# Attention units of eight heads and DMA transposes in a fused adaLN transformer layer on one NeuronCore

## The chip, the cores and the metric

The kernel runs on one core of a Trainium2 chip. The metric is the device time of one execution in microseconds (us). A core has a matrix engine (PE, with its weight loads shown as PEld), a vector engine (DVE), a scalar engine (ACT), a general engine (POOL), a queue engine that issues DMA transfers (SP), and 16 DMA engines that carry them. ACT can issue DMA transfers too, on a queue of its own.

## The reference

One transformer layer on 2,048 tokens of 1,024 features in bf16, with scales and shifts (`sa, ca, ga, sb, cb, gb`) made from a condition vector `c`. Attention has 32 query heads of 32 features and a single key and value head.

```
mod = silu(c) @ w_mod                       # six fields of 1024
h   = layernorm(x) * (1 + ca) + sa
q   = h @ wq (32 heads of 32); k = h @ wk; v = h @ wv      # one k and v for all heads
o   = softmax(q k^T / sqrt(32)) v
x   = x + ga * (o @ wo)
h   = layernorm(x) * (1 + cb) + sb
x   = x + gb * ((silu(h @ w1) * (h @ w3)) @ w2)            # 3584 hidden features
```

## The kernel before

**Tiles and blocks.** Tokens are cut into 16 tiles of 128 for the first norm and for keys and values, and into 8 blocks of 256 queries (`NB`, `B`). The 1,024 query features are 8 chunks `f` of 128, so a chunk holds four heads.

**Start.** For every token tile, `lnt1` takes statistics (bn_stats on DVE), makes 1/sigma on POOL, normalizes on ACT (tiles 0 to 7) or DVE (8 to 15) into one of three slots `XN`, transposes the tile on PE by eight 128x128 matmuls and evicts it to `HT` on ACT or DVE. `mod_cols` makes the first scale and shift from `w_mod` (tile `WM0`), `scale0` folds the scale into `wk`, `wv` and the first two chunks of `wq` (`WQ0S`), `k_bias` and `q_bias` make the biases that come from the shift. `k_proj(j)` makes the keys of 256 tokens (`KT`), `v_proj` the values, `q_proj` the query chunks (`QT`). The rest of `wq` (`WQ1`) is scaled in place on DVE once it has landed. All large loads are issued by SP, in an order written out by hand: x tiles 0-7, half of WM0 and the first chunks of `wq` first; then x tiles 8-11, the rest of WM0 (field 0), `WQ1`, x tiles 12-15; then `wo` (`WO`, it waits for `WQ1` to land) and chunks of `w_mod` (tile W2S in the profile).

**Attention.** A step works on one query chunk of a block (four heads) and two key tiles: eight score matmuls of 256 columns on four 32-row parts of PE (`s_exp`), then two exponentials of 128x1024 on ACT into a ring `U` of ten steps. A unit is one chunk, eight steps. `av` adds the 16 key tiles of exponentials on DVE (`pairs` adds two key tiles of two steps, then further additions halve what is left, tile PS), multiplies the exponentials with V (eight matmuls of 256 columns per step on four 32-column parts of PE) and the sums with ones (the denominators), and normalizes: a transpose, a copy, a reciprocal, a transpose back and a product, all on DVE. The result overwrites the query chunk in `QT`.

**The rest of the layer.** For each finished block `wo` multiplies with `wo`, adds x and takes the second norm, whose transposes are done by DMA for blocks 1 to 6; `slab` (14 per block) makes the gated hidden features, with a tanh on ACT and two products on DVE; `quarter` (4 per block) makes the output. This work on block n fills PE while the exponentials of block n+1 run.

**Order.** Nothing is ordered by hand after recording. `op` records an operation with its planned cost and what it reads and writes; `Placer` then lists operations engine by engine: of those that could start about now it takes the one with the earliest due time `vt`. `PLAN` holds one row for every 16 score steps: tolerances, and shifts of the due times by kind of operation. PE distinguishes three modes (scores `S`, attention-value `A`, dense `F`). Within an engine instructions run strictly in the placed order. All instructions are recorded by one helper, so the profile gives them all one line (L22), and tiles tell them apart.

Of the kernel before, what the change touches and what calls it, by code (L numbers as in the profile page):

```python
# [42 lines left out]
class Graph:  # L43
# [63 lines left out]
    def alias(self, new, old):  # L107
# [8 lines left out]
    (0.2, 0.03, 0.0, 0, 1.4,  # L116
     {"q/pe": -9, "slab/act": -80, "wo/dve": -71, "ln/pe": -112, "ln/act": 31, "k/pe": 3, "k/dve": 33}),
    (0.0, 0.12, 0.2, 1, 0.2,
     {"av/pe": -2, "q/pe": -9, "pair/dve": -2, "av/dve": -33, "slab/act": -18, "ln/pe": -57, "ln/act": 23}),
    (0.0, 0.16, 0.02, 0, 0.7, {"wo/pe": 106, "q/pe": -45, "q/dve": -74, "ln/pe": -118, "ln/dve": 4, "mod/pe": -24}),  # L120
    (0.0, 0.16, 0.02, 0, 0.7, {"wo/pe": 106, "q/pe": -45, "q/dve": -74, "ln/pe": -118, "ln/dve": 4, "mod/pe": -24}),
    (0.2, 0.24, 0.2, 1, 0.6, {"q/pe": 47, "mc/pe": 46, "ln/act": -12, "k/pe": 22}),
    (0.0, 0.12, 0.2, 0, 1.8,
     {"wo/pe": -44, "quarter/pe": 47, "q/pe": 33, "mc/pe": 36, "pair/dve": -14, "wo/dve": -1, "ln/act": -12,
      "k/pe": 22}),
    (0.0, 0.11, 0.2, 1, 1.5, {"q/pe": 47, "mc/pe": 46, "av/dve": 6, "ln/act": -12, "k/pe": 22}),
    (0.0, 0.11, 0.2, 1, 1.9, {"q/pe": -13, "mc/pe": 46, "av/dve": 4, "ln/act": -12, "k/pe": 22}),
    (0.0, 0.11, 0.2, 0, 3.4, {"wo/pe": 35, "an/dve": 55, "slab/dve": 1}),
    (0.0, 0.11, 0.2, 1, 1.4, {"av/dve": -11, "an/dve": 55, "slab/dve": 1, "q/dve": 9}),
    (0.0, 0.11, 0.1, 0, 2.4,  # L130
     {"wo/pe": 14, "slab/pe": 12, "quarter/pe": 3, "q/pe": -6, "av/dve": 18, "an/dve": 69, "slab/act": -1,
      "quarter/dve": -7}),
    (0.0, 0.11, 0.05, 0, 2.4, {"slab/act": 6, "wo/dve": 53}),
    (0.0, 0.11, 0.2, 0, 2.9, {"wo/pe": 46, "an/dve": 55, "slab/dve": -89, "q/dve": 67}),
    (0.0, 0.11, 0.2, 1, 1.3, {"wo/pe": -13, "pair/dve": 6, "an/dve": 55, "slab/dve": -89, "q/dve": 67}),
    (0.0, 0.11, 0.1, 1, 2.7,
     {"slab/pe": -132, "q/pe": 47, "mc/pe": 46, "pair/dve": -13, "av/dve": 23, "slab/dve": -39, "slab/act": -20,
      "quarter/dve": -47, "ln/act": -12, "k/pe": 22}),
    (0.0, 0.11, 0.1, 1, 2.3,
     {"slab/pe": -132, "q/pe": 47, "mc/pe": 46, "pair/dve": -13, "av/dve": -84, "slab/act": -20,  # L140
      "quarter/dve": -47, "ln/act": -12, "k/pe": 22}),
# [3 lines left out]
    (0.0, 0.11, 0.2, 1, 1.3,  # L145
     {"slab/pe": -124, "q/pe": 47, "mc/pe": 46, "pair/dve": -24, "av/dve": -89, "an/dve": -26, "slab/dve": -39,
      "slab/act": -20, "ln/act": -12, "k/pe": 22}),
    (0.0, 0.11, 0.05, 1, 3.7,
     {"wo/pe": -5, "quarter/pe": 48, "pair/dve": -3, "av/dve": -2, "slab/act": -7, "wo/dve": 20}),
    (0.0, 0.11, 0.05, 1, 3.7,  # L150
     {"wo/pe": -5, "quarter/pe": 48, "pair/dve": -3, "av/dve": -2, "slab/act": -7, "wo/dve": 20}),
# [4 lines left out]
    (0.0, 0.11, 0.2, 1, 1.3,  # L156
     {"slab/pe": -124, "quarter/pe": 26, "q/pe": 52, "mc/pe": 46, "pair/dve": 13, "av/dve": -72, "an/dve": -26,
      "slab/dve": -39, "slab/act": -20, "quarter/dve": 35, "wo/dve": -6, "ln/act": -12, "k/pe": 22}),
    (0.0, 0.11, 0.05, 1, 2.6,
     {"slab/pe": -124, "quarter/pe": 26, "q/pe": 20, "mc/pe": 46, "av/dve": -89, "slab/dve": -39,  # L160
      "slab/act": -20, "quarter/dve": 35, "ln/act": -12, "k/pe": 22}),
    (0.0, 0.11, 0.05, 1, 1.4,
     {"slab/pe": -124, "quarter/pe": 26, "q/pe": 20, "mc/pe": 5, "av/dve": -89, "slab/act": -20,
      "quarter/dve": 35, "ln/act": -12, "k/pe": 22}),
    (0.0, 0.11, 0.2, 0, 1.6, {"wo/pe": 74, "pair/dve": 40, "av/dve": -2, "an/dve": 55, "slab/dve": -102, "q/dve": 6}),
    (0.0, 0.11, 0.2, 1, 1.4, {"wo/pe": -13, "pair/dve": 40, "av/dve": -2, "an/dve": 55, "slab/dve": -88}),
    (0.0, 0.11, 0.05, 1, 1.9,
     {"slab/pe": -124, "quarter/pe": -21, "q/pe": 20, "mc/pe": 46, "pair/dve": 43, "av/dve": -89,
      "slab/dve": -39, "slab/act": -20, "quarter/dve": 35, "ln/act": -12, "k/pe": 22}),
    (0.0, 0.11, 0.05, 1, 1.9,  # L170
     {"slab/pe": -124, "quarter/pe": -21, "q/pe": 20, "mc/pe": 46, "pair/dve": 43, "av/dve": -89,
      "slab/act": -20, "quarter/dve": 35, "ln/act": -12, "k/pe": 22}),
    (0.0, 0.11, 0.2, 0, 3.4, {"wo/pe": 61, "q/pe": -20, "pair/dve": 3, "slab/dve": -23, "wo/dve": 33}),
    (0.0, 0.11, 0.2, 1, 1.4, {"wo/pe": -5, "quarter/pe": 48, "pair/dve": -20, "av/dve": -27, "slab/act": -7}),
    (0.0, 0.11, 0.05, 0, 2.1,
     {"slab/pe": -124, "quarter/pe": -21, "q/pe": 20, "mc/pe": 46, "pair/dve": 43, "av/dve": -89,
      "slab/dve": -39, "slab/act": -20, "quarter/dve": 35, "q/dve": -75, "ln/act": -12, "k/pe": 22}),
    (0.0, 0.11, 0.05, 0, 4.0,
     {"slab/pe": -124, "quarter/pe": -21, "q/pe": 20, "mc/pe": 46, "pair/dve": 43, "av/dve": -89,
      "slab/act": -20, "quarter/dve": 35, "q/dve": -75, "ln/act": -12, "k/pe": 22}),  # L180
    (0.0, 0.11, 0.2, 0, 3.7,
     {"wo/pe": -4, "slab/pe": -43, "q/pe": 20, "mc/pe": 46, "pair/dve": 43, "av/dve": 55, "slab/dve": -39,
# [4 lines left out]
class Placer:  # L187
# [121 lines left out]
    def commit(self, n, e, k, start):  # L309
# [11 lines left out]
        if e == "sp" or n.dma is not None:  # L321
            self.t[e] = start + dur
            self.bw = max(self.bw, start + 2.6) + n.nbytes / n.bw
            n.fin = self.bw + 0.5
# [119 lines left out]
def build(nc, x_in, wq_in, wk_in, wv_in, wo_in, w1_in, w3_in, w2_in, c_in, wmod_in, out, S, D, F):  # L444
# [34 lines left out]
    RB = sb("RB", [P, 2, B], F32)  # L479
# [9 lines left out]
    RC = sb("RC", [P, 8], F32)  # L489
# [8 lines left out]
    Uf = U[:].rearrange("p a b c d -> p (a b c d)")  # L498
    HTf = HT[:].rearrange("p a b -> p (a b)")
# [16 lines left out]
    GP = HTf[:, o:o + 1024].rearrange("p (s x) -> p s x", s=2)  # L516
# [10 lines left out]
           W2f[:, 0:NC * 512].rearrange("p (c f) -> p c f", c=NC)]  # L527
# [48 lines left out]
    def x_dma(tt0, cnt, vt):  # L576
# [5 lines left out]
        dma("sp", dst, x2[tt0 * P:(tt0 + cnt) * P, :].rearrange("(t p) d -> p t d", p=P), ("XL", tt0),  # L582
            cnt * P * D * 2, writes=keys, vt=vt, bw=FAST)
# [8 lines left out]
    def wq_dma(f0, f1, key, vt):  # L592
        dma("sp", WQ[:, :, f0 * P:f1 * P], cp(wq_in)[:, :, f0 * P:f1 * P], key, (f1 - f0) << 18, writes=[key], vt=vt,
            bw=FAST)
# [61 lines left out]
    def lnt1(tt, vt):  # L656
# [13 lines left out]
        static = tt < 6  # L670
# [138 lines left out]
    def mod_chunk(i, vt):  # L809
# [4 lines left out]
        if i == 1:  # L814
            G.alias([("WMB", 1)], [("XS", tt) for tt in range(6, 10)])
# [31 lines left out]
    CYC = [(n, f, j) for n in range(NB) for f in range(NC) for j in range(NJ)]  # L847
    exps = {}

    def s_exp(c):  # L850
        G.tag = "s"
        n, f, j = CYC[c]
# [8 lines left out]
        op("pe", mm, 0.2184, reads=[("KT", j), ("QT", n, f)], writes=bk, vt=TOP + c, mode="S", post=0.171)  # L861
# [8 lines left out]
    def pairs(c):  # L870
        G.tag = "pair"
        m = c % NU
        op("dve", lambda: [lambda e: e.tensor_tensor(PS[:, c % NP:c % NP + 2], U[:, m:m + 2, :, 0, :],
                                                     U[:, m:m + 2, :, 1, :], ALU.add)], 1.12,
           reads=[("U", m + k, i) for k in range(2) for i in range(2)],
           writes=[("PS", (c + k) % NP) for k in range(2)], vt=c + 101.0, post=0.08)
# [348 lines left out]
```

## Time and profile before

| What | Value |
|---|---|
| Time, median of 3 runs | 1134.34 us (1134.11 to 1134.49) |
| The profiled execution: its own time | 1134.47 us |
| Its span in the trace | 1132.6 us |
| Exponentials on ACT | 1,024 of 128x1024, 964.3 us busy |
| DVE additions of exponentials (`pairs`) | 256 of 128x2048, 1,214 ns each |
| DVE additions of sums | 368 of 128x1024, 684 ns each |
| Input and weight traffic | 209.47 MB, 185 GB/s on average |
| Granted PE clock | full in all 40 slices |

Busy times of neighbouring instructions overlap in this profile: the interval from one start to the next on an engine is shorter than the duration of one (an exponential lasts 1,111 ns and starts 904 ns after the one before). Where the text speaks of a cost in a row of instructions, it means the interval. In a wait, the name behind the arrow is what the waiting engine's next instruction needed last.

### The profile page before, as it was taken

How to read it: one execution, taken by the hardware profiler on the slowest of the kernel's cores; microseconds unless marked ns; L12 is line 12 of the kernel's file. 1: busy time of each engine (PE TensorE's matmuls, PEld its weight loads, DVE VectorE, ACT ScalarE, POOL GpSimd, SP SyncE). 2: the span in 40 equal slices, each digit the busy share in tenths (PEclk: the TensorE clock that was granted, in tenths of full speed). 3: DMA queues.
4: the chain of work that ended last, by engine and by line, in shares of the span. 5: the costliest groups of instructions: out<-in, count | busy, mean ns of one | idle time of the engine just before them, and what ended most of it. 6: DMA issues, size and time to landing. Idle time of an engine off the chain costs nothing.

```text
span 1132.6 us, 34805 instructions
## 1 busy us (share of the span) xinstructions
PE 1113.1 (98%) x15600; PEld 754.6 (67%) x15600; DVE 951.9 (84%) x1544; ACT 1026.0 (91%) x1165; POOL 53.8 (5%) x95
## 2 busy tenths in 40 slices
PE   7999999999999999999999999999999999999998
PEld 6643546666577656776567756776577657766887
DVE  7888899989988888888988998888988988888442
ACT  6999999999999999999999999999999999996110
POOL 5100000000100001000100000000100000000000
PEclk9999999999999999999999999999999999999999
DMA  9500379665596667766596658765696559667793
GB/s 344 184 2 1 114 225 242 186 196 151 129 263 194 173 166 209 208 191 165 141 262 192 174 148 237 196 193 142 173 248 195 160 146 238 190 185 209 217 296 116
DMA packets 374292, 209.47 MB, mean 185 GB/s; under 512 B 17536, under 2 KB 365952, under 8 KB 374144
## 3 DMA queue, kind: packets, MB, share of 16 engines
q1 hardware_dynamic: 373712, 207.11, 65.8%
q8 instruction: 123, 2.02, 0.8%
q14 instruction: 25, 0.20, 0.1%
q10 hardware_dynamic: 432, 0.13, 0.0%
HBM read 199.89 MB, written 4.19 MB: 180 GB/s over the span
## 4 chain that ended last, share of the span: by engine, by line
PE 63%; ACT 31%; DVE 4%; DMA 1%; issue 0%; POOL 0%; SPq 0%; DVEq 0%
PE PB L22 47%; ACT U L22 30%; PE S L22 16%; DVE PS L22 2%; DMA W<-in_A_wq_dram 1%; ACT HT L22 1%; DVE HT L22 1%; DVE RB L22 0%; SPq L22 0%; DVE ST L22 0%; DVE W L22 0%; ACT XNB L22 0%; POOL PS L22 0%; DVE XNB L22 0%; POOL RS L22 0%
## 5 line engine op out<-in xcount | busy, mean ns | idle before, releaser
L22 ACT ACTIVATE U<-S 128x1024 bf16<-128x1024 f32 x1024 | 964.3, 1111 | 9.0 <-PE S L22 8.8
L22 DVE TENSOR_TENSOR PS<-U 128x2048 bf16<-128x2048 bf16 x256 | 309.7, 1214 | 11.7 <-ACT U L22 10.3
L22 DVE TENSOR_TENSOR PS<-PS 128x1024 bf16<-128x1024 bf16 x368 | 249.5, 684 | 4.7
L22 PE MATMUL PB<-QT,W 128*128 128x256 bf16 x1856 | 229.6, 273 | 0.0
L22 PE MATMUL S<-QT,KT 32*128 32x256 bf16 x4096 | 203.5, 273 | 6.0 <-ACT U L22 4.0
L22 PEld LDWEIGHTS PB<-QT,W 128*128 128x128 bf16 x1856 | 170.3, 98 | 46.6 <-issue 28.3
L22 PE MATMUL PB<-W2S,HT 128*128 128x256 bf16 x1512 | 189.1, 273 | 0.0
L22 PEld LDWEIGHTS PB<-W2S,HT 128*128 128x128 bf16 x1512 | 137.5, 98 | 42.4 <-issue 26.4
L22 PEld LDWEIGHTS S<-QT,KT 32*128 32x128 bf16 x4096 | 60.8, 92 | 132.7 <-ACT U L22 118.7
L22 PE MATMUL PB<-U,V 128*32 128x256 bf16 x4032 | 123.5, 273 | 0.0
L22 PE MATMUL PB<-QT,HT 128*128 128x256 bf16 x960 | 119.9, 273 | 0.0
L22 PEld LDWEIGHTS PB<-U,V 128*32 128x32 bf16 x4032 | 100.8, 97 | 18.8 <-issue 7.0
L22 ACT ACTIVATE HT<-PB 128x512 bf16<-128x512 f32 (+1 forms) x110 | 77.6, 707 | 32.0 <-PE PB L22 31.8
L22 PEld LDWEIGHTS PB<-QT,HT 128*128 128x128 bf16 x960 | 88.2, 98 | 23.7 <-issue 14.1
L22 PE MATMUL PB<-HT,W 128*128 128x256 bf16 (+1 forms) x576 | 101.8, 318 | 1.0 <-DVE HT L22 0.6
L22 DVE SCALAR_TENSOR_TENSOR HT<-HT,PB 128x512 bf16<-128x512 bf16 x102 | 69.4, 681 | 34.2 <-ACT HT L22 33.4
L22 DVE TENSOR_TENSOR HT<-HT,PB 128x512 bf16<-128x512 bf16 x102 | 69.5, 681 | 19.2 <-PE PB L22 18.5
L22 PEld LDWEIGHTS PB<-HT,W 128*128 128x128 bf16 x576 | 49.9, 97 | 38.1 <-issue 15.2
L22 DVE STREAM_TRANSPOSE RB<-PB 128x256 f32<-128x256 f32 x63 | 28.2, 448 | 38.7 <-PE PB L22 38.5
L22 PE MATMUL PB<-WO,QT 128*128 128x512 bf16 x232 | 57.3, 381 | 0.0
L22 POOL TENSOR_SCALAR RS<-MV 128x1 f32<-128x1 f32 x32 | 10.5, 329 | 969.9 <-DVE MV L22 966.9
L22 ACT ACTIVATE HT<-S 128x512 bf16<-128x512 f32 (+1 forms) x15 | 10.9, 736 | 30.5 <-PE S L22 30.5
(115 smaller groups left out, 675.2 us busy)
## 6 DMA issues: line engine op xcount, KB each, us to landing
W<-in_B_w_dram SPq DMA_DIRECT2D x150, 512.0 KB, 4.8
W2S<-in_B_w_dram SPq DMA_DIRECT2D x28, 1792.0 KB, 8.6
HT<-in_B_w_dram SPq DMA_DIRECT2D x74, 512.0 KB, 4.8
W2S<-in_w_mod_dram SPq DMA_DIRECT2D x8, 1024.0 KB, 7.2
X<-in_A_x_dram SPq DMA_DIRECT2D x8, 512.0 KB, 7.0
out_dram<-X SPq DMA_DIRECT2D x7, 512.0 KB, 9.1
U<-in_B_w_dram SPq DMA_DIRECT2D x1, 3584.0 KB, 13.5
W2S<-in_B_w_dram SPq DMA_DIRECT2D x1, 3584.0 KB, 15.2
```

What stands on the lines that cost most here:

```text
L22: return getattr(e, call[0])(*call[1], **call[2])
```

## The change

- **Units.** A unit becomes two neighbouring chunks (eight heads) of a block, 16 steps, and a step one key tile: four score matmuls of 512 columns, two exponentials as before, four attention-value matmuls of 512 columns. `av(g)` now handles half a unit (eight steps). The first half's product is copied to a buffer (`AVP`, later `GP`), the second half's added to it; denominators and normalization come once for a unit, on 512 columns.
- **Sums.** DVE adds the exponentials of two steps (128x2048), then such sums to each other, also as 128x2048, where it was 128x1024.
- **First norm.** Tiles 8 to 15 are transposed by a DMA from SP straight into `HT`, without PE and without eviction.
- **Loads.** WM0's field 0 is issued before x tiles 8-11. `WQ1` and x tiles 12-15 are issued by ACT, after it has normalized tile 7.
- **Order.** `PLAN` has new rows. The planner counts a DMA transpose as 4.1 us from its issue, whatever else is in the queue. The `w_mod` chunks and the first `w2` loads use the freed space a little differently.

In the placed order of the changed kernel, SP issues after the x tiles 8-11: transposes of tiles 8 and 9, the two halves of `WO`, a chunk of `w_mod`, the transpose of tile 10, another chunk, then the transposes of tiles 11 to 15. On DVE the norm of tile 13 comes before the key evictions of blocks 4 and 5, the scaling of `WQ` and all additions of exponentials.

The core of the diff (`PLAN` and the tables of buffers are left out):

```diff
-    x_dma(8, 4, -1893)
-    wm_dma(0, 0, -1892)
-    wm_dma(0, 1, -1891)
-    wq_dma(2, NC, "WQ1", -1890)
-    x_dma(12, 4, -1889)
-    wq1 = list(G.last["WQ1"])
+    wm_dma(0, 0, -1893)
+    wm_dma(0, 1, -1892)
+    x_dma(8, 4, -1891)
...
     def lnt1(tt, vt):
...
-        static = tt < 6
+        if tt >= 8:
+            o = op("sp", lambda: [lambda e: e.dma_start_transpose(HT[:, :, tt * P:(tt + 1) * P], XN[slot])], 0.5,
+                   reads=[("XN", slot)], writes=[("HT", cc, tt) for cc in range(NC)], vt=vt, dma=("HTL", slot), nbytes=1 << 18)
+            o.bw = -262144.0 / 1.0 * 1.0
+            return
+        static = tt < 4
...
-    CYC = [(n, f, j) for n in range(NB) for f in range(NC) for j in range(NJ)]
+    CYC = [(n, f, k) for n in range(NB) for f in range(0, NC, 2) for k in range(NTT)]
...
         def mm():
-            return [lambda e, g=g, kk=kk: e.matmul(
-                BANK[2 * r[g // 2] + g % 2][:, kk * B:(kk + 1) * B],
-                KT[32 * g:32 * (g + 1), (2 * j + kk) * P:(2 * j + kk + 1) * P], QT[32 * g:32 * (g + 1), n, f, :],
-                start=True, stop=True, tile_position=(32 * g, 0)) for kk in range(2) for g in range(4)]
+            return [lambda e, g=g: e.matmul(
+                BANK[2 * r[g // 2] + g % 2], KT[32 * g:32 * (g + 1), k * P:(k + 1) * P],
+                QT[32 * g:32 * (g + 1), n, f:f + 2, :].rearrange("p c q -> p (c q)"),
+                start=True, stop=True, tile_position=(32 * g, 0)) for g in range(4)]
...
+    def add(dst, a, b, ka, kb, vt, tag):
+        G.tag = tag
+        op("dve", lambda: [lambda e: e.tensor_tensor(PSW[:, dst], a, b, ALU.add)], 1.14, reads=ka + kb,
+           writes=psk(dst), vt=vt, post=0.08)
...
+        if hf == 0:
+            G.tag = "an"
+            op("dve", lambda b: [lambda e: e.tensor_copy(A, BANK[b])], 0.605, reads=[("av", g)], writes=ak, vt=vt, sess=s)
+            return
...
+        op("dve", lambda b: [lambda e: e.tensor_tensor(A, A, BANK[b], ALU.add)], 0.605, reads=[("av", g)] + ak,
+           writes=ak, vt=vt, sess=s)
...
     for j in range(2, 8):
+        if j == 4:
+            AL = list(G.last[("XN", 1)])
+            wq_dma(2, NC, "WQ1", -3000, "act", AL)
+            x_dma(12, 4, -3000, "act", AL)
+            wq1 = list(G.last["WQ1"])
```

More of the change, by code (lines that the diff above doesn't have):

```diff
@@ L868, in s_exp @@
                               writes=[("U", c % NU, i)], vt=c, post=0.083)
[L870 to L876, printed above, removed]
-    def level(u):
-        return 2 if u < 8 else 3
@@ L881, in av, with psk @@
[L881 to L894 removed]
+    def psk(s):
+        return [("PS", 2 * s), ("PS", 2 * s + 1)]
@@ new lines, in uk, with upair, fold @@
+    def uk(c):
+        return [("U", c % NU, i) for i in range(2)]
+    def add(dst, a, b, ka, kb, vt, tag):
+        G.tag = tag
+        op("dve", lambda: [lambda e: e.tensor_tensor(PSW[:, dst], a, b, ALU.add)], 1.14, reads=ka + kb,
+           writes=psk(dst), vt=vt, post=0.08)
+    def upair(dst, c):
+        add(dst, UW[:, c % NU], UW[:, (c + 1) % NU], uk(c), uk(c + 1), c + 101.0, "pair")
+    def fold(dst, src, c):
+        add(dst, PSW[:, dst], PSW[:, src], psk(dst), psk(src), c + 102.0, "av")
@@ new lines, in level, with sums @@
+    def level(w):
+        return 2 if w < 4 else 3
+    def sums(g):
+        w, c0 = g // 2, g * NJ
+        if g < SPLIT:
+            return []
+        if level(w) == 2:
+            for q in range(0, NJ, 4):
+                d = 2 * (g % 2) + q // 4
+                upair(d, c0 + q)
+                if d < 3:
+                    upair(3, c0 + q + 2)
+                    fold(d, 3, c0 + q + 2)
+                else:
+                    for c in (c0 + q + 2, c0 + q + 3):
+                        add(3, PSW[:, 3], UW[:, c % NU], psk(3), uk(c), c + 101.0, "pair")
+            return [2 * (g % 2), 2 * (g % 2) + 1]
+        d = g % 3
+        for q in range(0, NJ, 2):
+            upair(3 if q else d, c0 + q)
+            if q:
+                fold(d, 3, c0 + q)
+        if g % 2 and level(w) == 4:
+            fold((g - 1) % 3, d, c0 + 6)
+            return []
+        return [d]
@@ L895, in av, with avp @@
+    hold = {}
+    SPLIT = 0
+    DNP = W2f[:, 8 * D:9 * D].bitcast(F32)
+    def avp(n):
+        if n == 0:
+            return W2f[:, 0:D].bitcast(F32), ["AVP"]
+        return GP.bitcast(F32), [("GP", 0)]
+    def av(g):
+        n, f, hf = g // NC, g % NC // 2 * 2, g % 2
+        w = g // 2
+        s = Sess(False)
+        sl = sums(g)
+        hold[g] = sl
+        G.tag = "av"
         for q in range(NJ):
             def mm(b, q=q):
-                return [lambda e, h=h, kk=kk: e.matmul(
-                    BANK[b][32 * h:32 * (h + 1), 0:B], V[:, 2 * q + kk, :], U[:, (u * NJ + q) % NU, h, kk, :],
-                    start=(q == 0 and kk == 0), stop=(q == NJ - 1 and kk == 1), tile_position=(0, 32 * h),
-                    skip_group_check=True) for kk in range(2) for h in range(4)]
@@ L929, in av @@
-        op("dve", lambda: [lambda e: e.transpose(RB[:, 0, :].rearrange("p (a r) -> p a r", r=32),
-                                                 RC[:].unsqueeze(2).broadcast_to([P, 8, 32]))], 0.36,
+                return [lambda e, h=h: e.matmul(
+                    BANK[b][32 * h:32 * (h + 1), :], V[:, NJ * hf + q, :],
+                    U[:, (g * NJ + q) % NU, h].rearrange("p c q -> p (c q)"),
+                    start=(q == 0), stop=(q == NJ - 1), tile_position=(0, 32 * h),
+                    skip_group_check=True) for h in range(4)]
@@ new lines, in av, with md @@
+        if hf == 0:
+            G.tag = "an"
+            op("dve", lambda b: [lambda e: e.tensor_copy(A, BANK[b])], 0.605, reads=[("av", g)], writes=ak, vt=vt, sess=s)
+            return
+        sd = Sess()
+        ks = hold[g - 1] + sl
+        for x in ks:
+            def md(b, x=x):
+                return [lambda e, h=h: e.matmul(
+                    BANK[b][32 * h:32 * (h + 1), :], ONES[:, 0:32], PSW[:, x, h * 512:(h + 1) * 512], start=(x == ks[0]),
+                    stop=(x == ks[-1]), tile_position=(0, 32 * h), skip_group_check=True) for h in range(4)]
+            op("pe", md, 0.216, reads=["ONES"] + psk(x), writes=[("dn", w)], vt=-500 + g, mode="A", sess=sd, post=0.175)
```

245 lines of the change are left out of this document (125 added, 120 removed).

## Prediction

> **What bounds it now.** I read the busy table first, then the busy time by stage, the chain of waits of the start, and the DMA issues.
>
> ```profile
> PE 1113.1 (98%) x15600; PEld 754.6 (67%) x15600; DVE 951.9 (84%) x1544; ACT 1026.0 (91%) x1165; POOL 53.8 (5%) x95
> ```
>
> An average over stages. I cut the span where the first exponential of every 128 starts on ACT (one block of 256 queries):
>
> ```profile
> 30.61:56.30 25.69, 23.61 (x466) 16.89 (x465) 23.37 (x47) 25.54 (x30) 3.69 (x8) 1.00 0.50 170
> 56.30:153.63 97.33, 96.37 (x1339) 44.08 (x1336) 84.35 (x140) 97.33 (x107) 0.00 (x0) 1.00 0.17 56
> 153.63:279.34 125.71, 121.37 (x1824) 80.55 (x1821) 113.78 (x187) 124.91 (x144) 2.55 (x4) 1.00 0.74 199
> 279.34:405.49 126.15, 125.70 (x1794) 85.58 (x1793) 112.49 (x176) 124.78 (x144) 4.95 (x6) 1.00 0.70 189
> 1036.50:1132.60 96.10, 93.16 (x882) 80.04 (x880) 39.61 (x70) 8.36 (x14) 1.59 (x4) 1.00 0.81 223
> ```
>
> Columns: stretch, length, busy time of PE, PEld, DVE, ACT, POOL, clock, DMA. From 56 to 154 us ACT never rests: block 0 is bound by exponentials (0.904 us from start to start). From block 2 on PE and ACT are both full; the last 96 us are PE alone. What PE costs there is read from matmul starts:
>
> ```profile
> 333.86 0.40 PE L22 MATMUL S<-QT,KT 32*128 32x256 bf16 x8
> 334.19 1.92 PE L22 MATMUL PB<-QT,W 128*128 128x256 bf16 x16
> 336.05 0.40 PE L22 MATMUL S<-QT,KT 32*128 32x256 bf16 x8
> ```
>
> A score step takes 0.33 us, 16 dense matmuls 1.86 (0.109 each); both hold one switch of tile shape, about 0.11. The start is another regime:
>
> ```profile
> 30.61 3.76 ACT L22 ACTIVATE U<-S 128x1024 bf16<-128x1024 f32 x4
> ...
> 48.17 10.23 ACT L22 ACTIVATE U<-S 128x1024 bf16<-128x1024 f32 x11
> ```
>
> Thirteen exponentials take 17.56 us there (11.75 would do). The chain of waits from 34 to 50 us runs mainly through DVE (statistics, norms, scaling of WQ, pair sums). The DMA issues of that time, each with its time to landing (issued at 30.23, 31.19 and 32.49 us), and the transposes of later blocks:
>
> ```profile
> WO<-in_A_wo_dram SPq DMA_DIRECT2D x1, 1024.0 KB, 5.6
> W2S<-in_w_mod_dram SPq DMA_DIRECT2D x1, 1024.0 KB, 10.4
> W2S<-in_w_mod_dram SPq DMA_DIRECT2D x1, 1024.0 KB, 13.1
> QT<-XNB SPq DMA_TRANSPOSE x2, 3.1
> ```
>
> They land at 35.8, 41.6 and 45.6: what SP queues lands in order, 3 us a megabyte. The transposes' 3.1 us was measured with SP's queue empty.
>
> **Units of eight heads.** Exponentials keep number and shape. A score step becomes 4 matmuls of 512 columns for 8 of 256, attention-value steps likewise. The 512-column row starts every 0.215 us, two of 256 take 0.218: 0.003 us x 1,024 steps = 3 us less PE work. Counted in both orders, switches of tile shape are 1,102 for 1,106: nothing. On DVE the folds go from 6 of 1,024 elements (0.684 us) to 3 of 2,048 (1.214) per eight steps: 4.1 to 3.6 us. Two units' normalization was 2 x (0.448 + 0.424 + 0.198 + 0.442 + 0.418) = 3.9 us; now a copy and an addition of 512 columns (0.68 each, from the eviction row), two transposes (0.79, twice the row less its start), reciprocal 0.2, product 0.74: 3.9. Both hide beside ACT and PE; if DVE were the bound they would still be even.
>
> By the Trainium skill's "Perfetto Trace Analysis", Identifying the Most-Contended Engine, LDWEIGHTS busy share is the fair measure of a full PE; halving these loads takes about 86 of 755 us off it, so by that rule it should gain much. The trace disagrees: 64 attention-value matmuls start to next step in 1.86 us, which is their columns and one switch.
>
> **Loads.** WM0's field 0 moves ahead of x tiles 8-11. That load took 2.7 us of the queue (17.6 to 20.3), so WM0 lands at 23.1 instead of 25.8 and the x tiles at 25.8. From landing to first exponential was 4.8 us (25.8 to 30.6). Now the first step needs two query chunks: one projection (0.9), its eviction (0.48) and a bn_stats (0.61) that stands before it on DVE come in, partly beside the rest: I get 28.3, a gain of 2.3 us. WQ1 and x 12-15 leave ACT after norm tile 7 (about 24.5). Such issues took 0.37 to 1.57 us with room in the queue, up to 5.47 without. Behind them wait ACT's key evictions and the first exponential; with the short ones DVE's query chunk (27.5) covers it, with a long one 2 to 3 us of the gain go. I take the short: only x 8-11 is then in flight. WQ1 lands near 31.5, x 12-15 near 34.5 (before 30.2 and 32.7).
>
> **Tiles 8-15 by DMA.** Away go 64 PE transposes (0.056 us each, 3.6 us) and eight evictions, five of them on ACT after the first exponential (0.92 each); tile 7's eviction (0.92) and one more key eviction (0.45) now stand there: 3.2 us less of ACT. Added are eight transposes on SP and new waits: slots of XN are reused, so on DVE the norm of tile 13 waits for transpose 10 to land, 14 for 11, 15 for 12; behind them stand the key evictions 4 and 5, WQ's scaling and every pair sum. In the placed order SP issues T8, T9, WO (2 MB, only after WQ1's landing), 1 MB of w_mod, T10, another MB, T11 to T15. So:
> - norm 9 at 32.4, T9's issue (1.24) to 33.7; WO follows, its data from 35.6. Three megabytes: 44.5. T10 lands near 46. DVE reaches norm 13 near 41: 5 us blocked.
> - The next megabyte ends at 48.5; T11 50, T12 51.3. Norm 15 to 52, T15 issued then, landed 3.1 us later: 55.2.
> - ACT's order puts key eviction 7, which needs T15, before step 10's exponentials: 56.8. On PE 16 query matmuls (3.5 us) stand before score step 11 and need WQ's last scaling on DVE (58.4). Step 11's exponentials start at 62, where before the 23rd exponential started at 56.3: 5.7 us later, though ACT has less to do.
> Bounds: 3.1 us per transpose whatever is queued gives 55.3 for the 23rd (-1, by DVE's own work); if the transposes neither wait nor let the query matmuls come first, 51.8 (-4.5). Above, 3.1 us apiece in line gives +8. I take +5.7, by the rows that show SP's queue in order.
>
> The Trainium skill's "Advanced Engine Details and Errata", X-Bar Transpose (TRN2), says such transposes run as fast as ordinary DMAs, 350 to 400 GB/s: 0.7 us a tile as an estimate from it. The sum by it would be 2 us lower; the 3.1 us row is far longer, but is time to landing and not of the queue.
>
> **After the start.** Block 0 stays bound by ACT: no change. Dense 256-column matmuls by block, counted in both orders: block 1 582 for 574, block 2 604 for 672, block 3 668 for 672, blocks 4-6 672 each, block 7 690 for 660, tail 816 for 782. Block 2 loses 7.4 us of PE work, but ACT's 128 exponentials and 14 tanh (122.3 us at 0.904 and 0.477) and its usual 1.5 us of gaps hold it at 123.8: 2.3 gained. Block 1 -1 (64 small matmuls of 0.03 gone), 3 to 6 together -1.1, block 7 +2.9, tail 34 x 0.109 + 0.2 = +3.9. Sum +2.2 (between -2.5, the PE work alone, and +5).
>
> **Sum.** Span 1132.6, the profiled execution 1134.5 (1.9 around it; the median of the runs is 1134.3). 1134.5 + 5.7 + 2.2 = 1142.
>
> **Rivals.**
> - *Transposes are not held by the loads*, chance 0.20: landing 3.1 us after issue. Start -1, rest +2.2: 1135.5 (1133 to 1137). For it: all twelve measured ones took about 3.1. Against: none had a load ahead.
> - *Faster: the start runs at ACT's pace*, 0.20. With eight heads a key tile lasts two steps, so key block j is needed 3.6 us x j after the first exponential, where before it was 1.8 x j. If T10 lands before DVE reaches norm 13 (41 us; that decides), the pair sums come early, the 23rd exponential starts at 51.8 (-4.5) and block 2's lighter PE load ends in idle time that existed before too: rest -2.5. 1127.5 (1125 to 1132). Against: WO's two megabytes alone fill the queue to 41.6.
> - *Weight loads were not hidden*, 0.02: half of 171 us of PEld (rows 60.8 + 100.8 + 9.2) at four tiles side by side is 21 us: 1113 to 1121 with or without the start's loss. Against: the starts above. The page named under the first edit would have it so.
> - *Longer DVE additions (1.2 for 0.68 us) hold the tanh products* that free PSUM for PE, 0.01: half a microsecond on each of 112 slabs would be 56 us, 1198 at worst.
>
> **Numbers.** Forecast, 0.57: 1142, own range 1137 to 1147. A measurement of this kernel can tell about 0.2% (2.3 us) from no change. Slower: 0.57, 0.04 of the first rival, 0.01. Same: 0.14 of the first rival. Faster: 0.20, 0.02, 0.02. Range for eight in ten: down into the faster rival, 1130, and up to the +8 with the upper end of the rest, 1148.
>
> **What would show it.** Right: first exponential near 28; DVE idle before norms 13 to 15, ended by the DMA transposes; T10's landing 9 us or more after its issue; the 23rd exponential near 62; block 2 near 124 us; a tail 4 us longer. Wrong: transposes landing 3 us after issue among loads, the 23rd exponential before 56, or blocks other than 0 and 2 off by over 1 us.

## The result, and the profile after

The changed kernel takes **1154.05 us** (median of 4 runs, 1153.64 to 1154.84), the kernel before on the same chip 1134.41 (1134.11 to 1134.67). The ratio is 1.0174 (95% interval 1.0156 to 1.0192): 19.6 us slower. The forecast was slower too, but by 7.5 us, and 1154 lies outside its range. The profiled execution has a span of 1153.0 us.

The busy table of the page after:

```profile
PE 1113.6 (97%) x11123; PEld 682.4 (59%) x11152; DVE 948.5 (82%) x1230; ACT 1017.7 (88%) x1157; POOL 59.3 (5%) x97
```

Weight loads fell by 72 us of busy time (754.6 to 682.4) and the kernel became longer. By the Trainium skill's "Perfetto Trace Analysis", Identifying the Most-Contended Engine, that share, beside the MFU, is the one by which to judge the headroom of TensorE; here it went down while the time went up.

The busy time by stage after, cut at the first exponential, just ahead of the 23rd (which starts at 66.85), and then at the first exponential of each 128 (blocks 4 to 6, within 0.3 us of block 3, are left out). Columns: stretch, length, busy time of PE, PEld, DVE, ACT, POOL, granted clock, DMA share, GB/s.

```profile
28.95:66.81 37.86, 24.61 (x333) 14.37 (x333) 25.82 (x55) 22.65 (x27) 6.46 (x16) 0.77 0.83 213
66.81:164.86 98.05, 93.64 (x912) 38.12 (x924) 88.08 (x117) 97.69 (x108) 0.00 (x0) 1.00 0.19 65
164.86:289.48 124.62, 119.84 (x1223) 71.13 (x1224) 110.15 (x142) 124.29 (x143) 1.58 (x4) 1.00 0.71 194
289.48:413.68 124.20, 121.02 (x1180) 69.97 (x1181) 109.14 (x132) 124.20 (x143) 5.31 (x7) 1.00 0.64 172
413.68:540.71 127.03, 125.69 (x1244) 76.25 (x1245) 110.61 (x134) 124.66 (x143) 6.11 (x7) 1.00 0.71 187
922.21:1053.14 130.93, 129.66 (x1282) 80.28 (x1283) 111.08 (x135) 125.29 (x143) 6.46 (x6) 1.00 0.70 189
1053.14:1153.00 99.86, 97.01 (x883) 82.55 (x882) 41.48 (x71) 8.36 (x14) 1.59 (x4) 1.00 0.76 222
```

Set against before, in us:

| Stretch | Before | After | Difference |
|---|---|---|---|
| span's start to the end of block 0 | 153.63 | 164.86 | +11.2 |
| block 1 | 125.71 | 124.62 | -1.1 |
| block 2 | 126.15 | 124.20 | -1.9 |
| blocks 3 to 6 together | 504.61 | 508.53 | +3.9 |
| block 7 | 126.40 | 130.93 | +4.5 |
| tail | 96.10 | 99.86 | +3.8 |

So 11.2 us are lost in the start and 9.2 after it: two losses of about the same size.

The start first. ACT's exponentials in the timeline (start, length, what, how many, in brackets the idle time before and what ended it):

```profile
31.25 13.85 ACT L22 ACTIVATE U<-S 128x1024 bf16<-128x1024 f32 x15
55.48 1.94 ACT L22 ACTIVATE U<-S 128x1024 bf16<-128x1024 f32 x2 [10.38 <-PE S L22]
...
65.02 5.66 ACT L22 ACTIVATE U<-S 128x1024 bf16<-128x1024 f32 x6 [3.71 <-DVE PS L22]
```

ACT starts well, then stands still for 10.38 us, and once more for 3.71. What DVE and SP did meanwhile, from DVE's waits, SP's timeline and the landing of the transpose issued at 37.05 (tile 10):

```profile
DVE XNB L22 <- DMA HT<-XNB: 7.3, 1, 7.3
DVE PS L22 <- DMA HT<-PS: 3.2, 2, 2.3
```

```profile
36.35 0.65 SPq L22 DMA_DIRECT2D W2S<-in_w_mod_dram x1
37.05 8.23 SPq L22 DMA_TRANSPOSE HT<-XNB  x1
45.32 0.59 SPq L22 DMA_DIRECT2D W2S<-in_w_mod_dram x1
```

```profile
HT<-XNB SPq DMA_TRANSPOSE x1, 11.8
```

Issuing tile 10's transpose alone held SP for 8.23 us, and it landed 11.8 us after its issue began, at 48.87. Behind it DVE waited 7.3 us for the slot of tile 13. The chain of waits then runs through tile 11's landing (6.92), the keys and ACT, and from 60 us through DVE, and ends at the exponentials that start at 65.02:

```profile
45.96 6.92 DMA HT<-PS
...
57.92 0.47 ACT KT L22
58.40 1.84 ACT U L22 x2
60.26 1.23 DVE PS L22
...
63.86 1.14 DVE PS L22
65.02 2.85 ACT U L22 x3
```

The last link is the ring `U` of ten steps: step 10's exponentials overwrite what the pair sum that the chain has from 63.86 still has to read. Step 11's exponentials, of which the 23rd is the first, had a second wait that ended at nearly the same time. On PE its scores stand behind query matmuls:

```profile
62.81 3.40 PE L22 MATMUL PB<-HT,W 128*128 128x512 bf16 x15
66.14 0.39 PE L22 MATMUL S<-QT,KT 32*128 32x512 bf16 x4
```

After the start, blocks 3 to 6 lose 3.9 us. PE has as much to do in them as before (busy 503.5 us for 503.0) but stands idle for 5.0 us where it was 1.7, in pieces so short that its list of waits hardly has them. ACT's waits over these four blocks show more, before (405.49 to 910.10 us):

```profile
ACT U L22 <- PE S L22: 5.4, 4, 1.4
```

After (413.68 to 922.21 us):

```profile
ACT U L22 <- PE PB L22: 6.0, 4, 1.5
ACT HT L22 <- PE PB L22: 2.6, 4, 0.8
ACT U L22 <- PE S L22: 1.3, 4, 0.3
```

That is 9.9 us for 5.4. Most of it stands at one place in each block, 81 to 84 us behind its start. In block 4:

```profile
620.91 3.01 PE L22 MATMUL PB<-QT,W 128*128 128x256 bf16 x26
...
622.21 0.60 ACT L22 ACTIVATE HT<-PB 128x512 bf16<-128x512 f32 x1 [0.77 <-PE PB L22]
...
623.85 1.69 PE L22 MATMUL PB<-U,V 128*32 128x512 bf16 x28
...
624.30 4.69 ACT L22 ACTIVATE U<-S 128x1024 bf16<-128x1024 f32 x5 [1.49 <-PE PB L22]
```

PE is busy there, but between two score steps (620.58 and 625.48) it has 26 dense and 28 attention-value matmuls in a row; a tanh and then an exponential wait for them. In block 4 of the kernel before no two score steps start more than 2.3 us apart.

The matmuls themselves behave as predicted. In block 4 a dense group starts 0.33 us after the score step before it; its 16 dense matmuls and a switch now take 1.96 to the next step, 0.1 more than the 1.86 of before:

```profile
608.14 0.39 PE L22 MATMUL S<-QT,KT 32*128 32x512 bf16 x4
608.47 1.92 PE L22 MATMUL PB<-QT,W 128*128 128x256 bf16 x16
610.43 0.39 PE L22 MATMUL S<-QT,KT 32*128 32x512 bf16 x4
```

### The profile page after: what moved, and what is told of

It reads as the page before. It is cut to its first block, busy times and chain, and to the rows that moved or that the text cites. A ratio compares the mean times of both kernels' runs of the same rounds, so it can differ in the third digit from the quotient of the medians.

```text
span 1153.0 us, 25631 instructions
## 1 busy us (share of the span) xinstructions
PE 1113.6 (97%) x11123; PEld 682.4 (59%) x11152; DVE 948.5 (82%) x1230; ACT 1017.7 (88%) x1157; POOL 59.3 (5%) x97
## 4 chain that ended last, share of the span: by engine, by line
ACT 62%; PE 30%; DVE 4%; DMA 2%; SPq 1%; issue 1%; POOL 0%; DVEq 0%
ACT U L22 59%; PE PB L22 20%; PE S L22 10%; ACT HT L22 3%; DVE PS L22 2%; DMA W<-in_A_wq_dram 1%; DMA HT<-PS 1%; SPq L22 1%; DVE ST L22 1%; DVE HT L22 0%; DVE QT L22 0%; POOL PS L22 0%; DVE X L22 0%; DVE XNB L22 0%; ACT PS L22 0%
## 5 line engine op out<-in xcount | busy, mean ns | idle before, releaser
L22 DVE TENSOR_TENSOR PS<-PS 128x2048 bf16<-128x2048 bf16 x180 | 220.0, 1222 | 2.6
L22 PE MATMUL S<-QT,KT 32*128 32x512 bf16 x2048 | 202.5, 386 | 14.0 <-ACT U L22 10.6
L22 PEld LDWEIGHTS PB<-QT,W 128*128 128x128 bf16 x1808 | 164.8, 98 | 55.3 <-issue 34.4
L22 PE MATMUL PB<-W2S,HT 128*128 128x256 bf16 x1540 | 194.2, 273 | 0.0
L22 PEld LDWEIGHTS S<-QT,KT 32*128 32x128 bf16 x2048 | 51.4, 91 | 163.9 <-ACT U L22 158.4
L22 PE MATMUL PB<-U,V 128*32 128x512 bf16 x2048 | 129.8, 381 | 0.3 <-DVE X L22 0.2
L22 DVE TENSOR_TENSOR HT<-HT,PB 128x512 bf16<-128x512 bf16 (+1 forms) x127 | 86.6, 683 | 15.7 <-PE PB L22 13.6
L22 PEld LDWEIGHTS PB<-U,V 128*32 128x32 bf16 x2048 | 46.0, 96 | 58.0 <-issue 18.3
L22 POOL TENSOR_SCALAR RS<-MV 128x1 f32<-128x1 f32 x32 | 16.8, 524 | 974.1 <-DVE MV L22 974.1
L22 PE MATMUL PB<-WO,QT 128*128 128x512 bf16 x211 | 53.8, 381 | 1.3 <-issue 0.8
L22 DVE BATCH_NORM_STATS2 ST<-X 128x6 f32<-128x512 bf16 x44 | 28.4, 682 | 6.1 <-DMA X<-in_A_x_dram 5.6
```

What stands on the lines that cost most here:

```text
L22: return getattr(e, call[0])(*call[1], **call[2])
```

## The experiments

My theory after seeing this: the start loses about 10 us to loads that stand ahead of the transposes, and the units lose another 9 by themselves. Rivals: the transposes are slow in any case; the low granted clock of the start; the placed order (`PLAN`) that came with the change is bad and the units innocent. Any edit that the placer sees reorders everything behind it. So the runs are of two kinds: some keep every engine's placed order and move a few instructions in it by hand; the others got rows of `PLAN` made anew, by one search for a short order.

**1. Loads last, order kept.** On SP only:

```diff
+def ORDER(sp):
+    t15 = max(i for i, x in enumerate(sp) if x[0].dma and x[0].dma[0] == "HTL")
+    late = [x for x in sp[:t15] if x[0].dma[0] in ("WO", "WMB")]
+    return [x for x in sp[:t15 + 1] if x not in late] + late + sp[t15 + 1:]
```

> The changed kernel with the instruction order of every engine kept; only on SP the two halves of WO and the first two chunks of w_mod are issued after the transpose of tile 15 instead of among the transposes of tiles 10 and 11. Theory (the loads ahead of them hold the transposes up): tile 10's transpose lands about 4 us after its issue instead of 11.8, near 39 us; DVE's 7.3 us wait before the norm of tile 13 and 2.3 us before 14 are gone; the 21st exponential starts near 55.5 instead of 65.0; blocks 1 to 7 and the tail keep their lengths; total 1144 to 1146 (after: 1154.0). Rival 1 (a DMA transpose is slow by itself, or the ring of three slots of XN is too short): tile 10 still lands after 45 us, total within 2 us of after. Rival 2 (the start's loss is swallowed later, since block 1 is bound elsewhere): the 21st exponential comes 9 us earlier but the total gains less than 4.

1145.81 us (1145.19 to 1147.18), ratio to before 1.0096 (1.0079 to 1.0113): 8.2 us less than after. DVE's waits have no line for tile 13 any more, tile 10's transpose lands at 40.40, 4.95 us after its issue, those issued from 42 us on land 3.1 after issue, and block 0 is 9.2 us shorter (135.91 after):

```profile
29.03:155.75 126.72, 118.75 (x1256) 52.31 (x1255) 113.71 (x171) 120.23 (x133) 6.59 (x16) 0.97 0.40 114
```

Block 1 gives 1.3 of it back (125.88 for 124.62); blocks 2 to 7 and the tail are those of after within 0.3 us. The theory holds for the start, though block 0 still ends 2.1 us later than before (155.75 for 153.63). 11.4 us against before remain.

**2. The clock.** The page's clock row shows a dip. In the windows of the changed kernel the granted clock is the number behind POOL's:

```profile
38.00:40.00 2.00, 0.39 (x4) 0.10 (x4) 2.00 (x6) 2.00 (x3) 0.79 (x2) 1.00 1.03 370
42.00:44.00 2.00, 0.61 (x4) 0.11 (x4) 0.00 (x0) 2.00 (x4) 0.00 (x0) 0.50 1.06 388
46.00:48.00 2.00, 0.00 (x0) 0.00 (x0) 0.00 (x0) 0.00 (x0) 0.00 (x0) 0.50 1.19 91
58.00:60.00 2.00, 2.00 (x35) 0.93 (x32) 1.38 (x4) 2.00 (x3) 0.00 (x0) 1.00 0.02 4
```

PE was busy a fifth of the time from 38 us, and soon it was granted half its clock; 8 key matmuls then took 1.89 us for 1.05. So idle matmuls were put on PE:

```diff
+    for c, m in ((7, 72), (6, 6), (5, 6), (4, 6)):     # behind score step c, m matmuls
+        ... wait for the exponentials that free the bank; m times:
+        e.matmul(BANK[...][:, 0:256], IDENT[:], IDENT broadcast to 256 columns)
```

> The changed kernel with 90 extra matmuls of the identity (256 columns, results unused) on PE between score steps 4 and 7 and the key projection that waits, so that PE does not stand idle from 39 to 50 us. Theory (the low granted clock from 40.7 to 57.7 us costs little, because DVE and the DMA transposes are late): the granted clock stays at full, the 8-matmul key projections take 1.0 instead of 1.9 us, total 0 to 1.5 us less than after (1152.5 to 1154). Rival (the clock is a main part of the start's loss): 3 us or more less.

1155.82 us (1154.79 to 1156.27), ratio 1.0185 (1.017 to 1.02); the interval overlaps that of after. The clock stayed full until 53.8 us and was then at half for 3.4 us, where in the changed kernel it is at half for 17.1. The first key projection behind the wait took 1.04, but DVE still waited for the same transposes. No gain: the clock was a follower of the wait, not its cause. The Trainium skill's "TensorE: Matmul & The Clock Gate" (Terms) prices such a dip at the throttled time times the missing share of the clock: for the 17 us from 40.7 to 57.8 an estimate of 8.5 us. The run took 13.7 of these 17.1 us away, 6.8 us by that price, and shows no gain; a matmul that waits for a DMA does not get its operand sooner by a faster clock.

**3. Units alone.** The changed kernel with tiles 8 to 15 transposed on PE and the loads issued as before, rows of `PLAN` anew:

```diff
-        if tt >= 8:
-            o = op("sp", ... e.dma_start_transpose(HT[:, :, tt * P:(tt + 1) * P], XN[slot]) ...
-        static = tt < 4
+        static = tt < 6
```

> Units of eight heads alone: the changed kernel with the first norm's tiles 8 to 15 transposed on PE and all input loads issued by SP in the order of before. Because any edit reorders everything after it, its rows of PLAN were made anew for it, by a search for the shortest placed order. Theory (the units themselves cost later: from a block's last exponentials to its first slab there are more and longer DVE operations, the output matmuls held back to bridge that leave PE short in block 2 and come back in block 7 and the tail): first exponential near 30.6 and block 0 ending within 2 us of before (153.6), block 2 near 124, block 7 near 131, tail 98 to 100, total 1139 to 1143. Rival (the rows of PLAN that came with the change are at fault, not the units): blocks 3 to 6 at 126 or less, block 7 and tail as in before, total 1135 or less.

1146.47 us (1146.19 to 1147.48), ratio 1.0107 (1.009 to 1.0124), more than expected. Block 0 ends where it did before, at 153.70 (before 153.63), and everything is lost later. Its block 0, block 4, block 7 and tail:

```profile
32.06:153.70 121.64, 116.61 (x1228) 51.88 (x1243) 111.60 (x160) 121.59 (x135) 4.19 (x9) 1.00 0.24 79
...
531.12:658.67 127.55, 126.10 (x1254) 77.61 (x1255) 111.22 (x136) 124.90 (x143) 6.54 (x6) 1.00 0.70 186
...
912.89:1045.17 132.28, 131.05 (x1292) 81.37 (x1292) 110.96 (x135) 125.22 (x143) 6.04 (x6) 1.00 0.72 190
1045.17:1144.60 99.43, 96.40 (x871) 81.39 (x872) 41.52 (x71) 8.36 (x14) 1.59 (x4) 1.00 0.78 220
```

**4. One load moved in the kernel before**, rows of `PLAN` anew:

```diff
-    x_dma(8, 4, -1893)
     wm_dma(0, 0, -1893)
     wm_dma(0, 1, -1892)
+    x_dma(8, 4, -1891)
```

> The kernel before with one load moved: WM0's field 0 is issued ahead of x tiles 8 to 11, as in the change, with nothing else of it; its rows of PLAN were made anew by the same search (a control on that search: it should find an order as good as that of before). Theory (what the earlier first exponential gains is lost again inside block 0, where DVE and the later loads decide): first exponential near 28.3 instead of 30.6, end of block 0 within 1.5 us of 153.6, total 1132.5 to 1135.5. Rival (the gain is kept): end of block 0 near 151.3, total 1132 or less.

1134.91 us (1134.31 to 1135.96), ratio 1.0003 (0.9993 to 1.0012). First exponential at 28.31, as forecast; but block 0 took 127.97 us and ended at 156.28, 2.7 later than before (1.5 at most was expected), and block 1 gave that back (124.08). The earlier exponential is worth nothing here. For the search this is the control: on four-head units it comes back to the time of before.

**5. The start alone, mended**: units of four heads again, the change's start, WO and w_mod after the last transpose, and the planner told of the queue.

```diff
+    wq1 = list(G.last[("HT", 0, 15)])      # WO and w_mod wait for tile 15's transpose
-                n.fin = start + 2.6 - n.nbytes / n.bw + 0.5
+                self.bw = max(self.bw, start + 1.7) - n.nbytes / n.bw
+                n.fin = self.bw + 0.5
-    CYC = [(n, f, k) for n in range(NB) for f in range(0, NC, 2) for k in range(NTT)]
+    ... one chunk, two key tiles per step, and the sums and normalization of before
```

> The other half of the change alone, mended: units of four heads and steps of two key tiles as in before, with the change's start (tiles 8 to 15 transposed by DMA, WM0's field 0 ahead of x tiles 8 to 11, WQ1 and x 12-15 issued by ACT), WO and the w_mod chunks issued only after the last transpose has landed, and the planner told that DMA transposes queue behind other transfers. Rows of PLAN made anew by the same search. Theory (units and start cost separately: the start lost time only because loads stood ahead of the transposes, and four-head units keep the later blocks as they were): first exponential near 28.5, block 0 ending near 153 to 154, blocks 3 to 6 at 126.0 to 126.3, tail near 96, total 1130 to 1133, at least 0.1% less than before. Rival (the DMA transposes cost the start something even with an empty queue, as the 3.1 us to landing would): block 0 ending 2 us or more after 153.6, total 1136 or more.

**1133.35 us** (1132.58 to 1134.34), ratio 0.9989 (0.998 to 0.9998): the best measured here, though 0.1% is less than one should build on. Not all as expected: block 0 ended at 155.52, 1.9 later than before, which is close to what the rival wanted; blocks 1 and 2 won 2.4 back, so that the rival's total did not come. Block 4 and the tail are those of before:

```profile
531.09:657.18 126.09, 125.66 (x1794) 85.60 (x1793) 110.96 (x174) 124.73 (x144) 5.64 (x7) 1.00 0.71 189
...
1036.08:1132.10 96.02, 93.17 (x883) 80.10 (x880) 39.61 (x70) 8.36 (x15) 1.59 (x4) 1.00 0.78 223
```

**6. Eight-head units on the same mended start**, rows of `PLAN` anew.

> The changed kernel (units of eight heads) with the same mended start as the kernel beside it, rows of PLAN made anew by the same search, longer. Against the run with only WO and w_mod moved (1145.8) it tells what the order that came with the change had lost; against the kernel with four-head units it tells what the units cost. Theory (the units cost by themselves, whatever the order): 1138 to 1142; tail 98 to 100, block 7 above 130. Rival (only the order was bad): 1134 or less, with block 7 and tail as in before.

1143.68 us (1143.23 to 1144.02), ratio 1.0078 (1.0064 to 1.0092), above the expected 1138 to 1142. Of the 1145.8 of experiment 1 the new order saved 2.1; 10.3 us against experiment 5 are left, with block 7 at 130.80 and a tail of 99.54. The order that came with the change is at fault for the smaller part only.

**7. Split folds.** Experiment 6 with

```diff
-        add(dst, PSW[:, dst], PSW[:, src], ...)               # 128x2048
+        for i in range(2):
+            ... e.tensor_tensor(PS[:, 2 * dst + i], PS[:, 2 * dst + i], PS[:, 2 * src + i], ALU.add)   # 128x1024
```

> The same as the run beside it, with one edit: the additions that fold sums into sums on DVE are two of 128x1024 again instead of one of 128x2048 (the additions of two steps' exponentials stay 128x2048, as in before). Rows of PLAN made anew. DVE has 0.15 us more to do for each fold, but shorter operations between its urgent ones. Theory (the longer DVE additions delay evictions and products for which PE waits): 2 to 4 us less than the run beside it, blocks 3 to 6 0.4 to 0.8 us shorter each, while the slabs of a block still begin as late and block 7 and tail stay long. Rival (DVE's granularity does not matter): the same or longer.

1139.9 us (1138.36 to 1140.89), ratio 1.0044 (1.003 to 1.0058): 3.8 less than the run beside it, although DVE is busy 12.7 us longer (961.2 for 948.5). The blocks are not all as expected: block 1 is 2.6 shorter (125.00 for 127.56) and blocks 4 to 6 are 0.6 to 1.1 shorter (126.63, 126.19 and 125.95 for 127.27, 127.02 and 127.03), but block 3 is 1.1 longer; block 7 and tail stay at 131.11 and 100.39. In blocks 4 to 6 the one long stop of ACT is gone. Its waits there in experiment 6, then in this one:

```profile
ACT U L22 <- PE PB L22: 4.5, 3, 1.5
ACT HT L22 <- PE PB L22: 1.7, 3, 0.6
ACT U L22 <- PE S L22: 1.0, 3, 0.3
```

```profile
ACT U L22 <- PE S L22: 3.4, 9, 1.0
```

The shorter operations came together with another order of everything. That it matters how long one DVE operation is, and not how long all take, fits these numbers, but it is not shown apart from the order.

**8 and 11. The clock again**, on experiment 5: idle matmuls around score step 3, first 34, then 26 in better places.

> The kernel with four-head units and the mended start, every instruction in the same order, plus 34 idle matmuls of the identity (256 columns, results unused) on PE around score step 3, so that PE does not stand idle between 35 and 42 us, where its granted clock fell to half until 46.7 us. Theory (a low clock at the start costs little): the clock stays full, the key projections of 8 matmuls take 1.05 instead of 1.89 us, total 0 to 1 us less (1132.3 to 1133.4). Rival (the clock is what still holds the start back): 1.5 us less or more, 1131.8 or below.

> Four-head units with the mended start, the order of every engine kept, plus 26 idle matmuls of the identity on PE, now only after score steps 3 and 4 and the key projection behind them (in the run before they stood ahead of the query biases and pushed these from 32.6 to 34.9 us). Theory (a low clock at the start costs little): clock full or nearly, total 0 to 1 us less than without them (1132.3 to 1133.4). Rival (the clock still holds the start back): 1131.8 or below.

The first took 1136.68 us (1135.67 to 1139.05), ratio 1.0018: the clock stayed full until 51.6 us (it was at half from 39.6 to 46.4 in experiment 5), but the idle matmuls stood ahead of the query biases, which started at 34.94 for 32.63. A badly built run. The second took 1134.48, but from 1131.57 to 1136.46, ratio 0.9994 (0.9985 to 1.0003): inconclusive, with no gain in the median. Its runs differ in the clock: the four in which it was full throughout took 1131.57 to 1133.80 us, the seven in which it was at 0.997 or 0.998 took 1133.35 to 1136.46. Whether the dip costs that time or a longer wait brings the dip is not shown.

**9. The last two chunks of a block as four-head units**, otherwise experiment 7, rows of `PLAN` anew:

```diff
+    def wide(n, f):
+        return f < NC - 2
```

> The kernel with split folds and eight-head units, with one more edit: the last two query chunks of every block are processed as two units of four heads, as in before. Rows of PLAN made anew. Theory (the output matmuls held back, and with them the longer block 7 and tail, come from the late end of a block's last unit): about 95 output matmuls before the first slab instead of 160, block 7 near 125 to 126, tail near 97, total 1136 or less. Rival (the stock is only one face of it; in an order of mixed units DVE and PE lose in blocks 2 to 6 what block 7 and the tail give back): block 7 and tail as in before, but blocks 2 to 6 near 127, total 1138 to 1141.

1142.33 us (1142.05 to 1143.47), ratio 1.0065 (1.005 to 1.0081). This was meant for the long block 7 and tail. In the kernels with eight-head units a block's second norm comes late, and PE fills the gap before the block's first slab with output matmuls of the block before. For block 6: DVE's two norms (first and last start), and output matmuls (those that read W2S) from block start to first slab. Before:

```profile
L22 DVE TENSOR_SCALAR XNB<-X,MV,RS x2: 541/542/542, 800.7 to 805.8; 128x1024 bf16<-128x1024 bf16 x2
783.95:811.80 27.85, 12.06 (x97) 8.58 (x95) 0.00 (x0) 0.00 (x0) 1.00 0.57 140
```

After:

```profile
L22 DVE TENSOR_SCALAR XNB<-X,MV,RS x2: 539/540/542, 814.6 to 823.1; 128x1024 bf16<-128x1024 bf16 x2
794.97:835.80 40.83, 20.17 (x162) 14.43 (x160) 0.00 (x0) 0.00 (x0) 1.00 0.62 149
```

Experiment 9:

```profile
L22 DVE TENSOR_SCALAR XNB<-X,MV,RS x2: 540/540/541, 804.7 to 809.6; 128x1024 bf16<-128x1024 bf16 x2
787.54:815.60 28.06, 11.89 (x95) 8.36 (x93) 0.00 (x0) 0.00 (x0) 1.00 0.55 136
```

From block start to the last norm: 21.9, 28.1, 22.1 us; matmuls held back: 97, 162, 95 (in experiment 7, which this run edits, 27.6 us and 140). So the late norm and the stock of 65 do come from a block's last unit, and block 7 is back at 125.78. But the tail is 98.72, blocks 2 to 6 take 126.5 to 128.4, and the total is worse than experiment 7 and above what theory and rival expected. The rival is the nearer of the two: the stock is one face of the loss; without it, in the order found, the loss stands in the middle blocks.

**10. Loads among the transposes again**, on experiment 5, order kept:

```diff
+    i = rest.index(t[2])      # tile 10's transpose
+    return rest[:i] + early[:3] + rest[i:i + 1] + early[3:] + rest[i + 1:]
```

> The kernel with four-head units and the mended start, every engine's order kept, only SP's loads put back to where the change has them: both halves of WO and a chunk of w_mod ahead of tile 10's transpose, another chunk ahead of tile 11's. Theory (the loads among the transposes cost the start 8 to 10 us whatever the units): tile 10 lands 10 us or more after its issue, block 0 ends 8 to 11 us later (164 to 166), total 1140 to 1144. Rival (with four-head units the start has slack for it, or later blocks give it back): total below 1138.

1145.01 us (1144.63 to 1145.76), ratio 1.0091 (1.0077 to 1.0104): 11.7 more than experiment 5, a little above the expected span. Block 0 ends at 166.57, 11.0 later, tile 10's transpose lands 11.0 after its issue, and the later blocks are as in experiment 5. The start's loss does not need the eight-head units.

**12. The loads in ACT's queue**, the changed kernel, order kept:

```diff
+    e = [i for i, x in enumerate(lst["act"]) if x[0].tag == "s"][5]
+    lst["act"][e:e] = [(n, "act", fn) for n, _, fn in late[:3]]      # WO, WO, w_mod
```

> The changed kernel, orders kept; both halves of WO and the first w_mod chunk are issued by ACT (between its exponentials, near 35 us) instead of SP, so they are in another queue at the same time; the second chunk goes behind the transpose of tile 15 on SP. Theory (order within SP's queue and SP's own blocked issue are what held the transposes): tile 10's transpose issues near 35.5 in about 1.3 us and lands within 5 us, total 1144 to 1147 as with the loads last. Rival (the 16 DMA engines are shared, and 3 MB ahead delay a transpose whichever queue issued them): tile 10 lands 7 to 12 us after its issue, total 1149 to 1154.

1152.08 us (1151.93 to 1152.24), ratio 1.0153 (1.0138 to 1.0169). The rival was right; 2.0 us were saved against after. Two transposes were issued by SP at 32.66 (tile 9) and 35.12 (tile 10). Between the first and tile 8's stood no load of SP's, as in the changed kernel, where it landed 4.2 us after issue. With WO issued by ACT at 33.43 it took 8.6:

```profile
HT<-XNB SPq DMA_TRANSPOSE x1, 8.6
```

Tile 10 took 12.61 (11.82 in the changed kernel). It is not only the order within SP's queue that holds a transpose, but what is in flight on either queue. The Trainium skill's "DMA: Bandwidth & Descriptors", Issuing engines are not separate DMA queues, says that such transfers run on the same 16 DMA engines and interleave whoever issued them; this run agrees.

## Why the prediction was right and wrong

- **What bounds, first exponential, loads on ACT**: right. 28.95 for 28.3; WQ1 landed at 31.48 and x 12-15 at 35.29 (31.5 and 34.5), and the two issues took ACT 0.39 and 0.60 us. That the gain would survive was wrong (experiment 4).
- **Tiles 8-15, the step that failed first**: the mechanism was the forecast one, norm 13 blocked by tile 10's transpose behind WO and w_mod; the size was not. The sum took 3 us a megabyte for three megabytes, to 44.5, and T10 at 46. But WO was issued at 35.17 for 33.7, since tile 9's transpose held SP for 2.21 us and not 1.24, and from there the three took 12.83 us for the sum's 10.8, to 48.00; the rows of before that the sum rests on have 11.4 (30.23 to 41.6). T10 landed at 48.87: 7.3 us blocked for 5. The last of the load moved beside the transpose (91 GB/s from 46 to 48 us); that this made it slow is not shown, since in experiment 1, with another megabyte and no transpose behind them, the same three also took 12.83 (47.37 to 60.20). T15 landed at 58.09 for 55.2, key eviction 7 came at 60.84 for 56.8, WQ's last scaling ended at 61.88 for 58.4. The end of the chain was the forecast one, query matmuls before step 11's scores, and a wait that the prediction left out beside it: two exponentials of step 10 stood 3.71 us for the ring `U`. Either alone holds the 23rd to about 66.5 us or later. It started at 66.85 for 62: +10.4 for +5.7. The rival by which loads do not hold the transposes is out (experiments 1 and 10); with nothing in flight the 3.1 us row was exact (experiment 1).
- **The X-bar rule** of the Trainium skill ("Advanced Engine Details and Errata", X-Bar Transpose (TRN2)): in line, tiles 11 and 12 landed 0.9 us apart (52.88 and 53.78) and 13 another 1.15 later (in experiment 1 tiles 10 and 11 landed 0.70 apart), near the 0.7 estimated from that page and far from 3.1 apiece. The price of a transpose was not the issue; the loads ahead were.
- **Blocks 1 and 2, tail**: right, -1.1 for -1, -1.9 for -2.3, +3.8 for +3.9. In block 2 ACT is busy for all of its 124.20 us; the forecast had 122.3 and 1.5 of gaps. (The five terms of the rest add up to +2.4, not +2.2.)
- **Blocks 3 to 6, the step that failed second**: -1.1 forecast, +3.9 measured; block 7 +4.5 for +2.9. Reading the dense matmuls of each block out of the order gave PE's work and not the waits that its order brings. PE's busy time over blocks 3 to 6 stayed where it was (503.5 us for 503.0), but PE stood idle 3.4 us longer, and ACT waited for PE 9.9 us for 5.4, mostly at the one place where 26 dense and 28 attention-value matmuls stand in a row; in block 7 ACT waited 5.5 us for 1.4. The prediction put these waits at nothing. Why the order has this row of matmuls is open, and so is how much of the loss it makes alone; in experiment 7 ACT has no such stop in blocks 4 to 6.
- **"Both hide beside ACT and PE; if DVE were the bound they would still be even"**: not borne out. The sums of DVE's time were nearly even (948.5 for 951.9), and splitting the folds, with an order made anew, still brought 3.8 us. The rival named for longer additions was given 0.01; that they hold the tanh products, as it said, is not shown.
- **Rivals**: that weight loads cost time is not borne out: a score step takes 0.33 us with 4 of them as with 8, and experiment 3 has 70 us fewer (684.2 for 754.6) and is 12 us slower. Faster by ACT's pace needed T10 before 41 us. In experiment 1 it landed at 40.40, but the 23rd exponential started at 57.74 and not at 51.8, so even the rival's start did not come; and the units' loss was not in its sum.
- **Not settled**: about 6.5 us between experiments 7 and 5. They stand in block 7 (131.11 for 126.34) and the tail (100.39 for 96.02), less the 3.8 by which block 0 ends earlier. The late last unit explains the long block 7, but taking it away moved the loss. The search may be what fails there.

## What to carry to other kernels

A DMA transpose inside a dependency chain cost here what was in flight ahead of it, on whatever queue; send large loads that nobody needs yet after it (8 to 12 us). When operations are merged or moved, sums of busy time per block are not enough: look for the longest stretch in which an engine that feeds another does something else (here 4.9 us of PE between two score steps, while ACT waited). And split a change into its parts with orders made anew for each: here one part was worth -1 us, once its loads were moved, and the other +10.

## What the hardware showed that was not expected

- Issuing one transpose of 256 KB held SP for 8.23 us while three megabytes were in flight, against 1.23 with no load in flight; loads on another queue delayed transposes as much (8.6 and 12.6 us to landing).
- After PE had been a fifth busy for about three microseconds its granted clock fell to half, from 40.7 to 57.8 us; idle matmuls on PE kept the clock for most of that time, and no gain clear of the noise was measured.
- Idle matmuls are not free: with 16 of them ahead of the query biases these started 2.3 us later (34.94 for 32.63), and that run took 3.3 us longer.
